# Four-layer attention and state-space stack on one core: first-forward kernel tiles in the attention core, a re-ordered first spectral block, and POOL's work re-dealt

## The chip, the cores and the metric

The kernel runs on one core of one Trainium2 chip. A core has five engines that run side by side, each from its own list of instructions: PE (matrix products; results go to PSUM, accumulation memory of eight banks), DVE (vector operations), ACT (scalar functions, copies and casts), POOL (general work; it can also issue DMA transfers) and SP (here it issues DMA transfers only). Engines wait for one another by semaphores. An engine takes its instructions strictly in order, so one that waits holds everything queued behind it on the same engine. "Evacuation" is a copy out of PSUM into on-chip memory by DVE or ACT, usually with a change of layout or type.

The metric is the time of one execution in microseconds (us), as the median of several runs; lower is better.

## The reference

The input x has 2048 positions of 512 channels in bf16. Two layers A and B alternate, A B A B, each with a layer-norm before it and a residual addition behind it. Both passes use the same weights.

```python
def _A_ref(x, wqkv, wo):                 # 32 heads of 16 channels
    q, k, v = ...                        # x @ wqkv, split
    idx = pos[:, None] - off[None, :]    # off = 0, 2, 4, ... 14
    logits = einsum("bhsd,bhswd->bhsw", q, kg) * scale   # masked where idx < 0
    attn = softmax(logits)
    return einsum("bhsw,bhswd->bhsd", attn, vg) @ wo

def _B_ref(u, A_re, A_im, B_re, B_im, C_re, C_im, log_dt, Dskip):
    P = exp((dt * A)[:, :, None] * l)              # 512 channels x 128 states x 2048 positions
    K = einsum("dn,dnl,dn->dl", Cc, P, dt * Bc).real
    Kf, Uf = rfft(pad(K, 4096)), rfft(pad(u, 4096))
    return irfft(Uf * Kf)[:2048] + u * Dskip

x = x + _A_ref(_layernorm(x)); x = x + _B_ref(_layernorm(x), ...)
x = x + _A_ref(_layernorm(x)); x = x + _B_ref(_layernorm(x), ...)
```

Layer A lets each position look at itself and at seven earlier ones, two apart. Layer B is a convolution over the whole length with a kernel K per channel, done with a Fourier transform.

## The kernel before

The stages follow each other, with overlaps at their seams; times are from the start of the span.

0 to 106 us, `k_gen` with ORDERK. The kernel K is computed once, from tables of powers (`A_t`, `B_t`) whose products are summed by PE over the states (`pk`), evacuated by ACT (`kgs`) and stored as bf16 to the scratch tensor `kd_dram` by `k_store` (L1331): four groups of six transfers, 24 in all. Interleaved with it is the front of the first layer A: layer-norm, transposes, and the projections of k and of the first q. It works on a reduced set of 641 positions; `k_load` later expands them to 2048.

106 to 186 us, the first attention core, `LayerA.core` with CORE0. A letter is one step; q runs over four quarters of the positions, ft over four quarters of the channels:

- `m` is a DVE product of q and k (`prod`, L342), `l` its sum on PE (L350 and L354), `x` the maximum (DVE), `e` exponentials (ACT), `r` the reciprocal of the sum (two ACT operations), `n` the normalization (DVE), `T` a transpose;
- `v` is a value projection on PE with its ACT evacuation (L400), sixteen in all. After the fifteenth and the sixteenth, two transfers each shift copies of v by rows (L403) for the window; those of the first are ahead of all the rest in the queue;
- `q` is a projection of q (L223) with its ACT evacuation (L225);
- `P` is a product of the weights and the values (`pav`, L467; DVE), `S` and `V` its sum over the window (PE, then an ACT evacuation), `O` the output projection with the residual (PE, ACT), and `b`, `d`, `a`, `f` are the layer-norm that follows, the input `u` of layer B.

The digits and capitals in CORE0 are steps of the coming block: `0` the index arithmetic of a table of sines (`indices`, eight iotas and eight multiplications of 128 x 512 int32 on POOL, L736 and L737); `2` to `5` the sines on ACT, stored to `g2_dram`; `1` and `6` the loads of the two channel halves of K (`k_half_load`); `8` and `9` one row's addition of Dskip on DVE (`k_half_fix`); `A` to `H` the copies of K into `k_perm` on ACT or DVE (`k_part`); `w` the load of a 4 MB table of Fourier factors, `w2_dram`, in four transfers (`load_w2`, L598).

186 to 241 us, the first spectral block, `FftB.run` with ORDER0. The Fourier transform of 4096 is factored into two steps. `K` and `U` are tiles of the first forward step of the kernel and of the input (`f1`: 16 matrix products of 128 x 64 outputs, one evacuation L798 of 128 x 1024, by ACT where the token ends in A, by DVE where it ends in D). Sixteen tiles of each exist, eight per half of the channels, and a half's spectrum is the 16 KB tile `a1s` (per partition). `k` and `u` are the second step (L809 or L816; the evacuation of `k` by the token's letter, that of `u` by ACT, L867). `m` is the DVE product of the spectra (`u_mult`); it also stores the kernel's spectrum to `kf_dram`, from which the second block loads it again. `y` and `Y` are the first inverse step, `w` and `z` the second, with a residual addition.

Seven steps are left over from the first core and are put in behind the first seven K tiles after the first, in the order LATE0: the end of one layer-norm group and its four rows on POOL (`a`), statistics of the rows 14 and 15 (`s`, `t`), their gathering (`g`), the reciprocal (`r`), the last group and its four rows on POOL (`b`), and two masks (`m`).

241 to 270 us, ORDERF: the end of the block's second half, with the front of the second layer A. 270 to 352 us, the second attention core with CORE1; there `w` loads the same table again. 352 to 397.5 us, the second spectral block with ORDER1, which makes only the input's spectrum.

What sets the order. The strings are executed token by token, and every instruction of a token goes behind the earlier ones of its engine: DVE, ACT, PE and SP have exactly the order of the strings, in the generator POOL too. After that POOL's instructions are placed by the compiler's own scheduler. Nearly all loads and stores of `before` are issued by SP, so a transfer that waits in SP's list holds the ones behind it. The `kr` pool holds the two halves `k_rl0` and `k_rl1` and the Dskip row until the core's end, `krctx2.close()`.

The lines which the steps below speak of most:

```python
dsk = krp.tile([1, D], BF16, name="dskip")
nc.sync.dma_start(dsk[:], ins["Dskip"].partition_broadcast(1))
...
late = la.core(x_sb, u, lnp, CORE0, ev, 3)
late["m"] = C["masks"]
krctx2.close()
...
fb.run(ORDER0, u, k=kp, late=[late[c] for c in LATE0.split()])
```

Of the kernel before, what the change touches and what calls it, by code (L numbers as in the profile page):

```python
# [10 lines left out]
ACT = mybir.ActivationFunctionType  # L11
ALU = mybir.AluOpType
# [8 lines left out]
P = 128  # L21
# [57 lines left out]
NCOL = (2, 2)  # L79
PRELOAD = (slice(0, 0), slice(5, 16))  # L80
# [119 lines left out]
class LayerA:  # L200


    def __init__(self, tc, nc, consts, lnst, A_wqkv, A_wo, layer, xnT, nq):
# [11 lines left out]
        self.ps_l = self.wv = None  # L215
# [143 lines left out]
    def core(self, x_sb, u, lnp, order, ev, nprod=0):  # L359
# [9 lines left out]
        with ExitStack() as c2:  # L369
# [17 lines left out]
            def pq_tile():  # L387
                return ps_q.tile([P, 512], F32, name="pq", tag="pq")

# [187 lines left out]
            if l == 0:  # L577
                out_proj(15)
                return {"a": lambda: [u_end(8), u_apply(8, range(8, 12), "pool")], "s": lambda: x_stats(14), "t": lambda: x_stats(15),
                        "g": lambda: u_aggr(12, 16), "r": lambda: u_rstd(12),  # L580
                        "b": lambda: [u_end(12), u_apply(12, range(12, 16), "pool")]}
# [11 lines left out]
    def load_w2(self, w2_dram):  # L593
# [3 lines left out]
        for c in range(4):  # L597
            self.nc.sync.dma_start(self.w2[:, c * 32:(c + 1) * 32, :], w2_dram[:, c * 32:(c + 1) * 32, :])  # L598
# [128 lines left out]
def build_g2(nc, tmp, p21, g2_dram, room):  # L727
# [4 lines left out]

    def indices(h):
# [13 lines left out]
class FftB:  # L747
# [38 lines left out]
    def spectrum(self, g, key):  # L786
        if g == (key == "ua"):
            return self.gtile("a1s")
# [832 lines left out]
```

## Time and profile before

| | |
|---|---|
| time, median of three runs | 399.32 us (399.11, 399.32, 401.1) |
| the profiled execution: time, span | 399.32 us, 397.5 us |
| mean granted clock of PE | 0.983 |
| busy: PE | 344.0 us (87%) |
| busy: DVE | 378.7 us (95%) |
| busy: ACT | 328.6 us (83%) |
| busy: POOL | 54.4 us (14%) |
| DMA | 54.17 MB, 62322 packets, mean 136 GB/s |

The span reaches from the first to the last instruction of the trace; the time of the execution is 1.8 us longer. "Busy" counts an engine's arithmetic instructions. In a row of busy groups stand the line, the engine, the operation, its output and inputs by name, their shapes, the count, the busy time and the mean of one in ns, and then the idle time of the engine ahead of them with what ended it. In a row of the timeline stand the start in us, the duration, the engine, the line and the instruction; "x3" means three in a row with their time together. A row of the table by stage has the window, its length, and the busy time and count of each engine. A row of DMA issues has the tile, the queue, the count, KB of each and the median time from issue to landing.

### The profile page before, as it was taken

To read this page: it belongs to the slowest core of one execution; us is meant where nothing else is said; L and a number is where in the kernel's file an instruction comes from. 1 tells how busy PE (TensorE), PEld (TensorE's weight loads), DVE (VectorE), ACT (ScalarE), POOL (GpSimd) and SP (SyncE) were. 2 spreads that over 40 slices of the span, in tenths; PEclk is the share of its full clock that TensorE was granted. 3 is DMA by queue.
4 is the path that set the end of the run, shared out by engine and by line. 5 is a ranking of instruction groups with operands and counts; after the bars stand their busy time and mean duration, and the time that the engine had idled before them with its cause. 6 is when DMAs were issued, how large, how long until landed. Compare 5 with 4: busy or idle time off the path is not lost.

```text
span 397.5 us, 14823 instructions
## 1 busy us (share of the span) xinstructions
PE 344.0 (87%) x6510; PEld 236.8 (60%) x6556; DVE 378.7 (95%) x452; ACT 328.6 (83%) x585; POOL 54.4 (14%) x75
## 2 busy tenths in 40 slices
PE   3855589799999979889998889999999998887895
PEld 2221237477535667657887888543456676566885
DVE  6999999999999999999999998979999999989994
ACT  7999989999566588988999987675566889989974
POOL 9303000000399302001500000100000001000000
PEclk9998869999999999999999999999999999999999
DMA  7953610314114754278137485820153037504506
GB/s 213 399 155 48 71 54 2 92 29 95 41 42 120 205 181 151 73 243 347 63 123 265 177 293 164 295 77 1 41 159 93 5 119 309 162 3 142 181 11 207
DMA packets 62322, 54.17 MB, mean 136 GB/s; under 512 B 33869, under 2 KB 50738, under 8 KB 60978
## 3 DMA queue, kind: packets, MB, share of 16 engines
q1 hardware_dynamic: 62250, 53.22, 43.7%
q8 instruction: 51, 0.84, 0.9%
q14 instruction: 13, 0.11, 0.1%
q10 hardware_dynamic: 8, 0.00, 0.0%
HBM read 30.15 MB, written 13.24 MB: 109 GB/s over the span
## 4 chain that ended last, share of the span: by engine, by line
PE 39%; ACT 25%; DVE 20%; issue 6%; SPq 4%; DMA 4%; POOL 1%; DVEq 0%; ACTq 0%; POOLq 0%
PE pq L398 7%; PE pq L223 5%; DVE pav L467 4%; PE pp L282 3%; ACT ln_junk L145 3%; PE pk L1309 3%; SPq L1414 3%; ACT ub L867 2%; PE pb L816 2%; PE pp L1247 2%; PE L L350 2%; DMA w_sb<-w_dram 2%; ACT ln_junk L1195 2%; ACT a1s L798 2%; DVE A_t L1143 2%
## 5 line engine op out<-in xcount | busy, mean ns | idle before, releaser
L467 DVE TENSOR_TENSOR pav<-attn,v_ext 128x4096 bf16<-128x4096 bf16 (+1 forms) x34 | 72.4, 2167 | 0.2
L342 DVE TENSOR_TENSOR prod<-qT,kT_ext 128x4096 bf16<-128x4096 bf16 x29 | 66.5, 2326 | 1.0 <-PE L L350 1.0
L1143 DVE TENSOR_TENSOR A_t<-A_t,pow_t 128x1024 bf16<-128x1024 bf16 (+4 forms) x46 | 38.1, 870 | 0.4
L492 PE MATMUL po<-ident,pav 64*128 64x64 bf16 x1664 | 29.1, 190 | 6.6 <-DVE pav L467 3.7
L492 PEld LDWEIGHTS <-pav 64*128 64x128 bf16 x1664 | 26.3, 95 | 14.3 <-DVE pav L467 10.3
L867 ACT CAST ub<-pb 128x1024 bf16<-128x1024 f32 x32 | 32.0, 1077 | 1.2 <-PE pb L816 1.2
L509 PE MATMUL pq<-wop,oT 128*128 128x512 bf16 x116 | 30.9, 380 | 2.3 <-issue 1.4
L816 PE MATMUL pb<-a1s,w_sb 128*128 128x64 bf16 x768 | 27.6, 193 | 5.0 <-ACT a1s L798 1.7
L398 PE MATMUL pq<-wv,xnT 128*128 128x512 bf16 x122 | 30.0, 380 | 0.3
L400 ACT CAST v_ext<-pq 128x512 bf16<-128x512 f32 x32 | 18.8, 587 | 13.4 <-PE pq L398 13.4
L816 PEld LDWEIGHTS <-w_sb 128*128 128x128 bf16 x768 | 24.9, 98 | 7.3 <-issue 5.2
L798 ACT CAST a1s<-pb 128x1024 bf16<-128x1024 f32 x29 | 28.1, 1057 | 0.8 <-PE pb L809 0.8
L1309 PEld LDWEIGHTS <-A_t 128*64 128x64 bf16 (+1 forms) x512 | 21.7, 103 | 5.6 <-issue 1.2
L1309 PE MATMUL pk<-B_t,A_t 128*64 128x84 bf16 (+1 forms) x512 | 23.6, 201 | 1.5 <-ACT kgs L1317 1.0
L225 ACT CAST qT<-pq 128x512 bf16<-128x512 f32 x24 | 14.1, 587 | 13.1 <-PE pq L223 13.1
L1247 PE MATMUL pp<-xnT,kT_ext 128*128 128x512 bf16 x87 | 22.8, 384 | 1.5 <-ACT kT_ext L1252 0.4
L798 DVE CAST a1s<-pb 128x1024 bf16<-128x1024 f32 x19 | 22.6, 1215 | 1.4 <-PE pb L809 1.3
L223 PE MATMUL pq<-xnT,kT_ext 128*128 128x512 bf16 x89 | 23.2, 380 | 0.4
L1111 PE MATMUL pt<-ws,ident 128*128 128x512 f32 x16 | 11.5, 811 | 13.7 <-ACT ws L1098 13.3
L398 PEld LDWEIGHTS <-xnT 128*128 128x128 bf16 x128 | 11.7, 98 | 14.7 <-issue 2.1
L509 PEld LDWEIGHTS <-oT 128*128 128x128 bf16 x128 | 11.8, 98 | 13.1 <-ACT oT L494 1.9
L809 PE MATMUL pb<-F1c,xnT 128*64 128x128 bf16 x256 | 17.8, 219 | 1.5 <-ACT ub L867 0.6
(274 smaller groups left out, 904.4 us busy)
## 6 DMA issues: line engine op xcount, KB each, us to landing
w_sb<-w_dram SPq DMA_DIRECT2D x8, 1024.0 KB, 7.8
w_dram<-xnT SPq DMA_DIRECT2D x1, 4096.0 KB
kf_ring<-kf_dram SPq DMA_DIRECT2D x13, 256.0 KB, 4.4
kf_ring<-kf_dram SPq DMA_DIRECT2D x26, 128.0 KB, 3.6
v_ext<-v_ext SPq DMA_DIRECT2D x4, 784.0 KB, 6.1
x_blk<-in_A_x_dram SPq DMA_DIRECT2D x4, 512.0 KB, 4.2
kT_ext<-in_A_wqkv_dram SPq DMA_DIRECT2D x4, 512.0 KB, 9.5
x_sb<-in_A_x_dram SPq DMA_DIRECT2D x4, 512.0 KB, 5.6
```

Source lines behind the costliest of these rows:

```text
L223: nc.tensor.matmul(pq[:], lhsT=self.wqk[:, dt, ft * P:(ft + 1) * P], rhs=self.xnT[:, dt, q * 512:(q + 1) * 512], start=(dt == 0), stop=(dt ...
L342: nc.vector.tensor_tensor(pr, self.qT[q][:, ft].unsqueeze(1).to_broadcast([P, W, 4, P]), kap, ALU.mult)
L398: nc.tensor.matmul(pp[:], lhsT=xnT[:, dt, a * P:(a + 1) * P], rhs=wv[:, dt, :], start=(dt == 0), stop=(dt == NDT - 1))
L467: nc.vector.tensor_tensor(pv[:, i], attn[:, n % 4].unsqueeze(2).to_broadcast([P, W, DH // parts, H]), vap, ALU.mult)
L492: nc.tensor.matmul(po[:, h, 0, i * nt + ft, :], lhsT=pvf[rows, i, w, ft * P:(ft + 1) * P], rhs=ident[rows, rows], start=(w == 0 and ft + i ...
L509: nc.tensor.matmul(pw[:], lhsT=oT[:, ftp, :], rhs=self.wo[:, ftp, :], start=False, stop=(ftp == NDT - 1), skip_group_check=ahead)
L798: (self.nc.scalar.copy if eng == "act" else self.nc.vector.tensor_copy)(dst, src)
L816: nc.tensor.matmul(p2[:, j, :], lhsT=self.w2[:, ec * EC + j, :], rhs=a1s[:, ec * EC + j, :], start=True, stop=True)
L867: nc.scalar.copy(ub[:], p2)
L1143: return lambda: nc.vector.tensor_tensor(*args)
L1247: nc.tensor.matmul(pps[kind, b, ft][:], lhsT=la.wqk[:, dt, c:c + P], rhs=la.xnT[:, dt, b * 512:(b + 1) * 512], start=(dt == 0), stop=(dt = ...
L1309: nc.tensor.matmul(o, lhsT=lhs, rhs=Bt[:, ri, c * CH + ql].rearrange("p b g -> p (b g)"), start=(not half and j % 4 == 0 and ri == 0), sto ...
```

## The change

Five things change together.

1. Four of the sixteen first-forward tiles of the kernel spectrum (KEARLY = 4) are made inside the first attention core. A new step `*` in CORE0 (`k_f1`) makes half a tile: eight matrix products into one PSUM bank of the pool that the core's projections use, `pq`, and one ACT copy of 128 x 512 into `a1s`. Eight `*` stand near the end of CORE0. ORDER0 has the twelve other K tiles. `a1s` lies now in the `kr` pool: one 16 KB tile holds both halves of the loaded K, then `a1s` of the kernel, then that of the input ("a1u"); the pool is closed after the block. With both halves in one tile, `1` and `6` stand side by side in CORE0.
2. The late layer-norm steps are tokens of ORDER0 (`a`, `s`, `t`, `g`, `r`, `e`, `c`, and `q` for the masks) in place of LATE0. The eight rows are single tokens: c4 on DVE, c5 on ACT, the other six on POOL.
3. The multiplications of the index arithmetic move from POOL to ACT: `0` is only the eight iotas, and the new steps `W`, `X`, `Y`, `Z` are two ACT operations each, in CORE0.
4. Transfers: half of the kernel's stores (groups 0 and 2, twelve of 24) are issued by POOL; the stores to `kf_dram` are issued by POOL, at the kernel's second step and not at the product; the table `w2_dram` is loaded in sixteen transfers in place of four, four per `w` token, with four `w` in CORE0 and in CORE1.
5. ORDERK, ORDER0, CORE0 and CORE1 are written in another order. The steps of ORDERK and of CORE1 are the same but for the three more `w` in CORE1. In ORDER0 DVE evacuates 6 K and 8 k tiles (before: 7 and 9), ACT 6 and 8 (9 and 7).

The diff, cut to its core:

```diff
 ORDERK = """
-sibCCiisbisCCCiiMMbsGiCMMiMMbbMMsTbGiiscbbccMMbiTisbTTbGGGcGTTTiTTGiiTTTsGbibbGGGasTcMMMMaiiaaaa
-aasMMTiillWaTlbyMMwMyyayMMaMMMbattseeMMMiiMMMMkkMMMMMkkbKHqqKaqqppaaQadxaUUUUUUUkkllxUWppaQUUKlq
-UqyUUUqqyyHyQxttkkTTTTTpdeeKTTTTQT3qqqqaaQkkQaakkKTaallqxqpWEQx333KxlTTykkkppTkyyyxxHtUUeKUUtppl
-kUUeUKkxkkUWpUlzKzzzxkkttKkeKekpUUUUUKkkkkUUUEUUxUKEqxppKooxqXkxkQpKkkoXXKpZZZxx
+CisibCsiibsCCCbiiisMCMMMMMMibbGcTsbiiGsMMcbbbMciiGsTTTTbbTTiiTTasTiiGGGcbbTTTbcMGGGsMMaMaaaaaaii
+sTTGGlliiWMMlbsMMyyyyibiwMMMtteeqqMMMMbQdMMMMMMkkaaKMMkMMkakMakHKqKqaaaqaUpUUpQUUUqUllUWxxplpyyy
+ayUQkkxKttdqHaeUUUUUTqeaQqqqQxaaTaqT33TTTapkkTTTKpTa3QllWqqTlTxxykykTTKyQppkyxH3lkktkeUUxWKUUtpU
+lxzzppzEzektKxxkkkKEKteepkkkkKKkkkUUkUUUUUUEKKUoUUUUkkkoKkoUUpxxqqKQppxXXXpZZxxZ
 """
 ORDER0 = """
-KD KA KA KA KD KA KD KA KD KA KD kA KA kD KA KD UA KD UA UA UD KA kA kD kA UD UA UD UA kD kA kD u UD
-u u UA m m m UA u u UD u UA m kD UA kD UA m m u UA u m kA u kD u m kD u kD kA kA yA m YA m yD u yA u
-m m m u u yA m m u YA m yA w000D yD yA YD yA w010D YA yD yA
+q a c0 s KD c1 KA KD t g KA KD KA r c3 e c7 KD KA c4D c2 c6 c5A kA kD kA kD kA KA KD UA KD UA UA UD
+KA UD UA UD UA kD kA u kD u UD m UA UA kA UD UA u m kD kA m u u kD m u UA m UA UA m kD u u u m kD u
+kA kA m m m u u u m m yA YA yD u m m u u m yA yA YA m w000D yA yD yA YD yA YA yD yA w010D
 """
-LATE0 = "a s t g r b m"
...
 CORE0 = """
-vmvvvlmqlxmvvvemlvqrlmqvnTmlvxqqlmevlrvmmvvvvnPllPqxmSqTeO0mPlVrP15SOS2PnOPVPOSml4qOOlb3mV78lPPC
-SOdxS6eOrPSPPOSnwaOPSBPOSaOS9bOfAPdbFPOtVftEGDSaafaOH
+mmvv0lvvmxvvllveqqrvYmmlnlmmvqTvvlWxvvvevmvrZq16XPllPqn5Sqml2mq4VTO3xPPSPl8qOmSPOV7ePOS9lOrVPmOn
+SPOOmSllwPBxEPADOGSeOSCrPFwHOwwn*SP****bPS*ObPSdaaf*fdOVbO*aafPSttaO
 """
 CORE1 = """
-0vm2m1llqqq3mmlqvlmmvvvllvxemmqvrvllqqnTvvmmxlqvvvvvmlvPPeqlrmqmlxSqnqSmTPPOOSelSPPpOSrOSmOOlPPS
-mppSOOnlPlppxSeOPwpbbrVPddffaSfOOPnVPpfPSpOSPpafbOSOppPttSdfafaaO
+0mv12m3llmmqqqlqvlvmmvxvllmvevqrmvnllqqTvvmmlqlxmmvPPvvvvveqlmlqxmqSrnOSTpPPOlSeSrPOSOPSPPOSqlpO
+SpmmOlOplnpPSxPeObbPdrpwVffaSfdOOPnVPPpfSpOSPpObafPSwOtppSdfwafwtaOa
 """
+KEARLY = 4
...
     def load_w2(self, w2_dram):
-        for c in range(4):
-            self.nc.sync.dma_start(self.w2[:, c * 32:(c + 1) * 32, :], w2_dram[:, c * 32:(c + 1) * 32, :])
+        def piece(i):
+            for c in range(4 * i, 4 * i + 4):
+                self.nc.sync.dma_start(self.w2[:, c * 8:(c + 1) * 8, :], w2_dram[:, c * 8:(c + 1) * 8, :])
+        return iter([lambda i=i: piece(i) for i in range(4)])
+
+    def w2_next(self, w2_dram):
+        if self.w2_parts is None:
+            self.w2_parts = self.load_w2(w2_dram)
+        next(self.w2_parts)()
...
+    def iotas():
+        for h in range(4):
+            for k in range(2):
+                g = gi[h][:, k * 4 * P:(k + 1) * 4 * P]
+                nc.gpsimd.iota(g.rearrange(...), pattern=[[8, 4], [128, P]], base=32 * h, channel_multiplier=0)
+
     def indices(h):
         for k, bias in enumerate((16384.0, 32768.0)):
             g = gi[h][:, k * 4 * P:(k + 1) * 4 * P]
-            nc.gpsimd.iota(g.rearrange(...), pattern=[[8, 4], [128, P]], base=32 * h, channel_multiplier=0)
-            nc.gpsimd.tensor_scalar(g, g, p21, bias, ALU.mult, ALU.add)
+            nc.scalar.activation(g, g, ACT.Identity, scale=p21, bias=bias)
...
     def kf_load(self, n):
             for h in range(2):
                 sync.dma_start(kc[h::2, 1], kc[1 - h::2, 0])
+            self.nc.gpsimd.dma_start(self.kf_dram[g, ec].rearrange("p r q e -> (p r) (q e)"), kc[:, 0].rearrange("p q e -> p (q e)"))
             return
...
     def u_mult(self, g, ec):
         if self.tag == 0:
-            self.nc.sync.dma_start(self.kf_dram[g, ec].rearrange("p r q e -> (p r) (q e)"), kc[:, 0].rearrange("p q e -> p (q e)"))
             self.free.append(kc)
...
-                    nc.sync.dma_start(dst, sr)
+                    (nc.sync if g % 2 else nc.gpsimd).dma_start(dst, sr)
...
     def k_half_load(h):
-        kr = krp.tile([P, NA, D // 2], BF16, name=f"k_rl{h}")
-        k_load(tc, nc, kr, kd, hs)
-        krs[h] = kr
+        if h == 0:
+            krs["both"] = krp.tile([P, 2, NA, D // 2], BF16, name="k_rl", tag="kr")
+        krs[h] = krs["both"][:, h]
+        k_load(tc, nc, krs[h], kd, hs)
...
+    def k_spectrum(name="a1s"):
+        return krp.tile([P, P * DQG], BF16, name=name, tag="kr")[:]
+
+    def k_f1():
+        i = krs["n"] = krs.get("n", -1) + 1
+        if i == 0:
+            krs["a1s"] = k_spectrum().rearrange("p (e q) -> p e q", q=DQG)
+        p1 = la.pq_tile()
+        for j in range(4):
+            lhs = kp[:, i * 4 + j].rearrange("p a r -> p (a r)")
+            for half, m in enumerate((C["F1c"], C["F1s"])):
+                nc.tensor.matmul(p1[half * 64:(half + 1) * 64, j * P:(j + 1) * P], lhsT=lhs, rhs=m[:], start=(j == 0), stop=True, skip_group_check=True)
+        nc.scalar.copy(krs["a1s"][:, :, i * 4:(i + 1) * 4], p1[:].rearrange("p (q e) -> p e q", q=4))
...
-    late["m"] = C["masks"]
-    krctx2.close()
+    late["q"] = C["masks"]
...
+    fb.S[0]["ka"], fb.cnt["K"], fb.one = krs["a1s"], KEARLY - 1, k_spectrum
     with tc.manual_schedule(engines=MAN):
-        late["."] = lambda: None
-        fb.run(ORDER0, u, k=kp, late=[late[c] for c in LATE0.split()])
+        fb.run(ORDER0, u, k=kp, more=late)
     fb.c_mid.close()
+    krctx2.close()
```

More of the change, by code (lines that the diff above doesn't have):

```diff
@@ L388, in pq_tile @@
                 return ps_q.tile([P, 512], F32, name="pq", tag="pq")
+            self.pq_tile = pq_tile
             def q_proj(q, ft):
@@ L761, in __init__ @@
         self.nkf = 0
+        self.nk = self.one = None
         g2p = self.c_grp.enter_context(tc.tile_pool(name=f"b{tag}_g2", bufs=1, reuse_waits="tile"))
@@ L787, in spectrum @@
         if g == (key == "ua"):
-            return self.gtile("a1s")
+            return self.one("a1u") if self.one else self.gtile("a1s")
         if self.pair is None:
@@ L935, in i2_cols, with run @@
             nc.scalar.copy(xr, p4[:])
-    def run(self, order, u, done=lambda g, t: None, k=None, late=(), more={}):
-        late, cnt = list(late), self.cnt
+    def run(self, order, u, done=lambda g, t: None, k=None, more={}):
+        cnt = self.cnt
         src = dict(K=("ka", k), U=("ua", u))
-        if not cnt:
+        if self.nk is None:
             self.nk, self.nm = (0, 0) if k is not None else (NG * NEC, 0)
@@ L967, in run @@
                 if op == "K":
-                    if n > 0 and late:
-                        late.pop(0)()
                     if n == NG * NQT - 1:
```

21 lines of the change are left out of this document (10 added, 11 removed).

## The prediction

> **What bounds the kernel now.** I read the page's busy times first, then the busy times by stage, then what VectorE (DVE) waited for, and then the lines of the stretch that the change touches.
>
> ```profile
> span 397.5 us, 14823 instructions
> PE 344.0 (87%) x6510; PEld 236.8 (60%) x6556; DVE 378.7 (95%) x452; ACT 328.6 (83%) x585; POOL 54.4 (14%) x75
> 106.00:140.00 34.00, 33.27 (x389) 16.80 (x388) 33.52 (x20) 20.04 (x35) 26.12 (x16) 1.00 0.46 120
> 140.00:186.00 46.00, 41.50 (x1063) 30.18 (x1074) 45.45 (x44) 40.16 (x89) 3.01 (x1) 1.00 0.58 191
> 186.00:244.00 58.00, 52.36 (x1521) 47.51 (x1521) 56.32 (x70) 53.68 (x61) 6.41 (x9) 1.00 0.56 195
> 0.00:106.00 106.00, 78.75 (x740) 45.85 (x753) 100.33 (x162) 97.13 (x193) 16.16 (x47) 0.94 0.44 111
> 270.00:352.00 82.00, 75.67 (x1521) 46.67 (x1532) 80.42 (x67) 62.88 (x137) 1.02 (x1) 1.00 0.33 108
> DVE prod L342 <- PE L L350: 1.0, 2, 0.5
> DVE kn L798 <- PE pb L816: 0.7, 2, 0.5
> ```
>
> The stage rows give window, length, then busy time of PE, PEld, DVE, ACT, POOL. DVE is the engine without slack: 135.3 of 138 us busy from 106 to 244 us, the first attention core and the first spectral block, where nearly all of the change lies. No wait of DVE there is longer than 0.5 us. So what leaves DVE's list shortens the span, as long as ACT and PE still deliver on time. They have little to give: PE is full in the first 34 us (33.3 busy), ACT in the last 58 (53.7 busy). Only ACT before 140 us is idle, 14 of 34 us.
>
> **The change part by part.** The sum goes against the profiled execution, 397.5 us of span and 399.32 us of time, which is the median of the three runs.
>
> (1) Early first-forward tiles and the re-dealt evacuations. The block order has twelve K tiles for sixteen: one DVE evacuation of a K tile less (seven to six), three of ACT less (nine to six). Of the second-step evacuations DVE has one less (nine to eight), ACT one more. Late layer-norm rows: POOL six for eight, DVE and ACT one more each.
>
> ```profile
> 194.92 3.61 DVE L798 CAST a1s<-pb 128x1024 bf16<-128x1024 f32 x3
> 184.97 1.06 DVE L197 TENSOR_SCALAR xnT<-x_sb,ln_rstd,ln_nb 128x512 bf16<-128x512 bf16 x3
> 193.49 5.60 ACT L798 CAST a1s<-pb 128x1024 bf16<-128x1024 f32 x6
> L195 ACT ACTIVATE xnT<-x_sb,ln_nb,ln_rstd 128x512 bf16<-128x512 bf16 x3 | 2.4, 816 | 0.0
> L400 ACT CAST v_ext<-pq 128x512 bf16<-128x512 f32 x16 | 9.4, 586 | 6.9 <-PE pq L398 6.9
> 160.00:186.00 26.00, 22.77 (x51) 1.00 0.66 222
> ```
>
> In rows an evacuation follows the next after 1.13 to 1.20 us on DVE and 0.93 on ACT. DVE: 2 x 1.13 - 0.33 = 1.93 us less. ACT in the block: 3 x 0.93 - 0.93 - 0.82 = 1.0 us less. The eight half tiles add 8 x 0.59 = 4.7 us of ACT at the end of the core (row of the equal-sized evacuation of v_ext). From 160 to 186 us ACT has 26 - 22.8 = 3.2 us free, so up to 1.5 us of it could stick out there, and the block takes 1.0 of that back; I count 0, with 1.5 us as the upper end. The matmuls are the same in number and only move.
>
> (2) The index arithmetic goes from POOL to ACT.
>
> ```profile
> 112.63 7.10 DVE L342 TENSOR_TENSOR prod<-qT,kT_ext 128x4096 bf16<-128x4096 bf16 x3
> 120.26 2.70 DVE L342 TENSOR_TENSOR prod<-qT,kT_ext 128x4096 bf16<-128x4096 bf16 x1
> 124.02 7.13 DVE L342 TENSOR_TENSOR prod<-qT,kT_ext 128x4096 bf16<-128x4096 bf16 x3
> 131.67 4.89 DVE L467 TENSOR_TENSOR pav<-attn,v_ext 128x4096 bf16<-128x4096 bf16 x2
> 142.02 6.68 DVE L467 TENSOR_TENSOR pav<-attn,v_ext 128x4096 bf16<-128x4096 bf16 x3
> 105.80 1.19 POOL L736 IOTA g_i<- 128x512 int32 x2 [67.48 <-PE pk L1309]
> 113.63 7.20 POOL L737 TENSOR_SCALAR g_i<-g_i,aux 128x512 int32<-128x512 int32 x2
> 125.21 7.01 POOL L737 TENSOR_SCALAR k_perm<-k_perm,aux 128x512 int32<-128x512 int32 x2
> L663 ACT ACTIVATE w_qi<-w_base,w_off,pk 128x512 int32<-128x512 int32 x1 | 0.9, 867 | 0.0
> ```
>
> While POOL multiplies (107 to 132 us) three products of equal size take 7.10 and 7.13 us against 6.68 later, one takes 2.70, and two 4.89 against 4.48: 0.42 + 0.42 + 0.45 + 0.41, about 1.7 us of DVE that should go, since the POOL multiplications go and only writing iotas stay. The Trainium skill ("SBUF — State Buffer", Who interferes with whom) says that a DVE instruction with two SBUF inputs contends with a GpSimd instruction that reads SBUF, not with one that only writes; the trace agrees, with the 2.70 us.
>
> ACT gets eight operations of 0.59 (v_ext's row) to 0.87 us (the one int32 row), 4.7 to 6.9 us in its 14 idle ones. But two of them stand ahead of a q evacuation. The new DVE list reaches its first PV product after one product and one normalization less than before: 131.67 - 2.28 - 0.60 - 1.25 (slow products) = 127.5 us, and the product that needs that q (two PV products of 2.23 and a normalization later) at 132.6. PE is full until then, so the last value projection comes only by what was taken from ahead of it: two q projections and a logit sum,
>
> ```profile
> 132.82 0.59 ACT L400 CAST v_ext<-pq 128x512 bf16<-128x512 f32 x1 [0.28 <-PE pq L398]
> 123.23 1.89 PE L223 MATMUL pq<-xnT,kT_ext 128*128 128x512 bf16 x8
> 127.06 0.94 PE L354 MATMUL L<-ind,prod 128*128 128x8 bf16 x32
> ```
>
> 2 x 0.86 + 0.8 = 2.5 us, to 130.3 for its evacuation. Then come the reciprocal (to about 132.3), two index operations and the q evacuation: 132.3 + 1.2 + 0.6 = 134.1 us, 1.4 us late. I charge DVE 1.4 us (2.0 with the 0.87 row, 0 if PE runs ahead of this count).
>
> (3) Half of the kernel stores go to POOL's queue.
>
> ```profile
> 106.37 15.81 SPq L1331 DMA_DIRECT2D kd_dram<-kgs  x24
> 123.28 0.23 SPq L1475 DMA_DIRECT2D dskip<-in_B_Dskip_dram  x1
> 123.57 0.69 SPq L403 DMA_DIRECT2D v_ext<-v_ext  x1
> v_ext<-v_ext SPq DMA_DIRECT2D x4, 784.0 KB, 6.1
> 121.84 2.35 POOL L737 TENSOR_SCALAR k_perm<-k_perm,aux 128x512 int32<-128x512 int32 x2
> ```
>
> SP keeps twelve of the 24 (7.9 us, to 114.3) and then stands at the dskip load, which waits for every kernel store, POOL's twelve too; behind it are queued the v_ext shift of the first PV products, the output weights, x and both kernel halves. No POOL-issued transfer is in this trace. Bounds for one: 0.66 us, SP's own issue (15.81 / 24), and 1.2 us, POOL's multiplication at its quickest (2.35 / 2), or 2.35 if it costs as much as a pair of them. I take the 0.66, being the same transfers. POOL starts after two iotas at 107.0; with some 2 us until the last lands, SP goes on at 107.0 + 12 x 0.66 + 2 = 117 us, and the shift lands at 117 + 0.3 + 6.1 = 123.4, before 127.5: no wait. At 1.2 us it lands at 129.8: 2.3 us. The Trainium skill ("DMA: Bandwidth & Descriptors", Latency and other measured facts) gives about 1 µs to the first byte of a POOL-issued transfer; by that as the price of one, an estimate, the shift would land at 127.4 and the sum stay as it is.
>
> (4) Both kernel halves are loaded back to back, and the second Dskip addition follows the first by 6.6 us on DVE, not 18.
>
> ```profile
> 133.43 0.64 SPq L403 DMA_DIRECT2D v_ext<-v_ext  x1
> 138.38 1.55 SPq L1398 DMA_DIRECT2D k_rl<-kd_dram  x1
> 139.97 11.78 SPq L1414 DMA_DIRECT2D k_rl<-kd_dram  x17
> DMA to landing us min/median/max: 3.5/5.3/7.1
> ```
>
> From the second shift to the end of one half SP needs 151.75 - 133.43 = 18.3 us, so the second half's first load goes at 130.3 + 18.3 = 148.6 and lands at 152.1 to 155.7. DVE wants it at 127.5 + 24.1 = 151.6, with the 1.4 us of (2) at 153.0: 0 to 2.7 us. I take 0: the 3.5 is that of the load with no x load ahead of it.
>
> (5) At nothing: the sixteen kf stores moved from SP to POOL (POOL has 6.4 us of work in the block's 58, and buffers come free earlier; the next layer's memset behind them on POOL is not early in its need); the w2 load in 32 smaller issues, 12 us more of SP in all, half in each layer. Its cover:
>
> ```profile
> 171.68 3.24 SPq L598 DMA_DIRECT2D w_sb<-w_dram  x4
> L816 PE MATMUL pb<-a1s,w_sb x302: 189/193/203, 191.9 to 215.0; 128*128 128x64 bf16 x151
> w_sb<-w_dram SPq DMA_DIRECT2D x8, 1024.0 KB, 7.8
> ```
>
> Issued to 174.9 and landed some 8 us on, it is first used at 191.9: 9 us of cover, against 6 us of added issue. The new orders of the kernel generator and of the second core hold the same instructions; DVE's idle time there is 5.7 and 1.6 us, so they can win 2 or 3 us at most and lose as much: 0.
>
> The sum: 399.3 - 1.9 - 1.7 + 1.4 = **397.1 us**.
>
> **The rivals.**
>
> POOL's queue holds SP (slower). Place: the dskip load. At a price p per transfer the shift lands at 107.0 + 12p + 8.4; the wait reaches the 3.6 us won at p = 1.32. At 1.6 it is 7.1 us, which takes the place of the 1.4: 399.3 - 3.6 + 7.1 = 402.8; at 2.35 it is 411.8. The first index operation on ACT waits for the same POOL queue. For it: dispatch by a software engine beside a busy DVE. Against: DVE runs two-input products then, not copies. The Trainium skill ("SBUF — State Buffer", the box on DVE blocking DMA) says that descriptors of POOL-issued transfers are not written while DVE is in a two-port mode, which it grants to copies, casts and tensor_scalar, not to tensor_tensor; by it the stores in the core are safe. No run here shows it yet. Chance 0.20.
>
> The gain arrives at DVE and is lost to ACT and loads (no change): ACT's 1.5 us of (1), the 0.87 row in (2) and 0.9 us of (4) at the median landing: 397.1 + 1.5 + 0.6 + 0.3 = 399.5; with one of them 398.5. Chance 0.13.
>
> A new order costs in the generator or the second core (slower): the generator runs ACT 97.1 of 106 us, so a DVE step moved 3 to 6 us ahead of the ACT step that it needs waits that long: 397.1 + 4.5 = 401.6. Against: the same steps, each moved little. Chance 0.12.
>
> The change not doing what it says: the half tiles share two PSUM banks with the output projections; if these then wait, nothing leaves the block early. This falls under the second rival.
>
> **How the numbers follow.** My forecast has 0.55, in 394.5 to 398.4 (the orders' 2.6 us below; 1.3 above). Within 0.5% of 399.3 (397.3 to 401.3), about what a measurement of this kernel can tell from no change, lie 0.12 of the forecast and the second rival; below it the other 0.43; above it the first and third, 0.32. Range: 394.0 to 404.0; what is left out is the tail of the first rival and better orders.
>
> **What would show it.** Products of 2.2 us at 107 to 132 us, none of 2.7. The dskip load on SP before 118 us, and a DVE wait ahead of the first PV product below 1 us. A DVE wait of about 1.4 us some 5 us later, on ACT's q. The first block's f1 evacuations ending some 2 us sooner relative to its first. Wrong if DVE waits on a v_ext shift or on the index operations for over 3 us, or if DVE's idle time from 0 to 106 us grows over 8 us.

## The result, and the profile after

The changed kernel takes 405.09 us (median of six runs, 403.62 to 407.03), the kernel before, in runs beside it, 401.17 us (399.11 to 404.58). The ratio is 1.0121 with a 95% interval of 1.0092 to 1.0150: slower by about 1.2%, where 397.1 us and a gain of 0.6% had been forecast. The profiled execution took 403.62 us, the shortest of its six and 4.3 us more than that of before.

The page's busy times, and then the busy times by stage of the changed kernel (window, length, then PE, PEld, DVE, ACT, POOL, granted clock, DMA share, GB/s):

```profile
span 401.8 us, 14890 instructions
PE 346.1 (86%) x6510; PEld 236.7 (59%) x6556; DVE 376.5 (94%) x451; ACT 335.7 (84%) x600; POOL 45.3 (11%) x93
140.00:186.00 46.00, 39.31 (x997) 27.60 (x1006) 39.60 (x37) 36.10 (x83) 3.02 (x1) 0.96 0.53 159
105.86:248.90 143.04, 128.25 (x2969) 95.06 (x2985) 132.46 (x129) 120.91 (x199) 27.03 (x43) 0.99 0.59 183
```

The last row goes from the first core product behind the generator to the first step of the second layer's layer-norm. The same stretch of the kernel before:

```profile
106.97:244.44 137.47, 126.65 (x2965) 94.62 (x2981) 134.77 (x130) 113.94 (x184) 34.57 (x25) 1.00 0.55 176
```

That is the account of the 4.3 us. The generator ends 1.11 us earlier. From there to 248.9 us DVE has 2.31 us less work (134.77 to 132.46), where 3.6 had been forecast, but stands idle 10.58 us in place of 2.70. The rest of the span is 0.16 us shorter. So work was saved, and 7.9 us of new waiting ate it. Most of the waiting falls in the first core: from 140 to 186 us DVE is idle 6.4 of 46 us, 0.55 before. What DVE waited for longest in the whole stretch, from the waits of the changed kernel (engine, line, what ended the wait; total, times, longest in us):

```profile
DVE attn L450 <- ACT rs L442: 3.8, 1, 3.8
DVE k_rl L1502 <- DMA k_rl<-kd_dram: 1.4, 1, 1.4
DVE z L814 <- PE pb L901: 1.3, 1, 1.3
DVE ln_bn L138 <- ACT x_sb L516: 0.8, 1, 0.8
```

The longest is followed back on the timeline, in order: ACT's last sine, SP's list, then ACT, PE and DVE (start, duration, instruction, and in brackets the idle time ahead of it and what ended it):

```profile
142.00 1.04 ACT L756 ACTIVATE k_perm<-g_i 128x1024 bf16<-128x1024 int16 x1
135.67 12.52 SPq L1428 DMA_DIRECT2D k_rl<-kd_dram  x17
148.24 0.61 SPq L1412 DMA_DIRECT2D k_rl<-kd_dram  x1
148.89 10.69 SPq L1428 DMA_DIRECT2D k_rl<-kd_dram  x17
159.69 2.62 SPq L757 DMA_DIRECT2D g_dram<-k_perm  x4
167.14 1.99 ACT L1506 COPY k_perm<-k_rl 128x1024 bf16<-128x1024 bf16 x2 [4.17 <-DMA w_sb<-w_dram]
171.00 1.89 PE L511 MATMUL pq<-wop,oT 128*128 128x512 bf16 x4 [3.75 <-ACT oT L496]
176.14 0.31 ACT L442 ACTIVATE rs<-ssum 128x128 bf16<-128x128 f32 x1
176.49 0.69 DVE L450 TENSOR_TENSOR attn<-ex,rs 128x1024 bf16<-128x1024 bf16 x1 [3.80 <-ACT rs L442]
```

The sines are made in the room of `k_perm`, and from there stored to `g2_dram`; the copies of the kernel may write `k_perm` only when those stores have landed. All four sines are ready at 143 us. Their stores stand on SP behind both kernel halves, 36 transfers, and go at 159.7 to 162.3 us; they take 4 to 4.9 us to land. ACT's first copy waits 4.17 us. The profile names a transfer of the table there, which landed at the same time; by the program the copy waits for the sine stores. Everything behind the copy on ACT waits with it: an evacuation that PE needs (3.75 us), the exponentials of the last quarter, and so DVE's normalization (3.80 us). And PE's clock drops behind its pause, shown by the same windows in steps of 2 us:

```profile
168.00:170.00 2.00, 0.00 (x0) 0.00 (x0) 2.00 (x5) 1.97 (x5) 0.00 (x0) 1.00 1.01 358
170.00:172.00 2.00, 1.00 (x3) 0.44 (x4) 2.00 (x2) 1.87 (x4) 0.00 (x0) 0.60 1.05 388
172.00:174.00 2.00, 2.00 (x55) 1.18 (x54) 0.69 (x3) 1.04 (x3) 0.00 (x0) 0.55 1.00 344
174.00:176.00 2.00, 1.87 (x38) 1.05 (x29) 0.00 (x0) 1.97 (x5) 0.00 (x0) 1.00 1.01 357
```

The granted clock (the third number from the end) was 0.55 to 0.60 for 4 us after the pause of 3.75 us, so PE's next matrix products took up to twice as long: four of 128 x 512 took 1.89 us, where the same four take 1.03 us at other times.

### The profile page after: what moved, and what is told of

Its sections match the earlier page's. It is cut to its first block, busy times and chain, and to the rows that moved or that the text cites. A ratio compares the mean times of both kernels' runs of the same rounds, so it can differ in the third digit from the quotient of the medians.

```text
span 401.8 us, 14890 instructions
## 1 busy us (share of the span) xinstructions
PE 346.1 (86%) x6510; PEld 236.7 (59%) x6556; DVE 376.5 (94%) x451; ACT 335.7 (84%) x600; POOL 45.3 (11%) x93
## 4 chain that ended last, share of the span: by engine, by line
PE 40%; DVE 26%; ACT 18%; issue 6%; DMA 5%; SPq 3%; POOL 1%; DVEq 0%; ACTq 0%; POOLq 0%
PE pq L400 7%; DVE pav L469 6%; PE pk L1323 4%; PE pq L223 4%; PE pp L1261 4%; PE pp L282 3%; DMA k_rl<-kd_dram 3%; DVE A_t L1157 3%; DVE B_t L1157 2%; ACT ub L883 2%; ACT a1s L814 2%; DVE prod L342 2%; PE L L350 2%; PE po L494 2%; PE pq L511 2%
## 5 line engine op out<-in xcount | busy, mean ns | idle before, releaser
L342 DVE TENSOR_TENSOR prod<-qT,kT_ext 128x4096 bf16<-128x4096 bf16 x29 | 65.2, 2283 | 0.7 <-PE L L350 0.5
L1261 PE MATMUL pp<-xnT,kT_ext 128*128 128x512 bf16 x88 | 24.9, 413 | 5.4 <-ACT xnT L1254 3.5
L832 PE MATMUL pb<-a1s,w_sb 128*128 128x64 bf16 x640 | 23.2, 193 | 4.7 <-ACT ub L883 1.3
L178 POOL TENSOR_TENSOR ln_rstd<-ln_rstd,ln_mh 128x4 f32<-128x4 f32 x2 | 4.1, 2028 | 144.3 <-DVE ln_msq L170 80.3
L814 DVE CAST a1s<-pb 128x1024 bf16<-128x1024 f32 x16 | 18.9, 1217 | 1.5 <-PE pb L825 1.3
L814 ACT CAST a1s<-pb 128x1024 bf16<-128x1024 f32 x20 | 19.4, 1041 | 1.0 <-PE pb L825 0.9
```

The costliest lines, as they stand in the source:

```text
L342: nc.vector.tensor_tensor(pr, self.qT[q][:, ft].unsqueeze(1).to_broadcast([P, W, 4, P]), kap, ALU.mult)
L814: (self.nc.scalar.copy if eng == "act" else self.nc.vector.tensor_copy)(dst, src)
L832: nc.tensor.matmul(p2[:, j, :], lhsT=self.w2[:, ec * EC + j, :], rhs=a1s[:, ec * EC + j, :], start=True, stop=True)
L1261: nc.tensor.matmul(pps[kind, b, ft][:], lhsT=la.wqk[:, dt, c:c + P], rhs=la.xnT[:, dt, b * 512:(b + 1) * 512], start=(dt == 0), stop=(dt = ...
```

## The experiments

The theory after reading the two traces: SP's list. With both halves loaded back to back, the sine stores start 8 us later than in the kernel before, and ACT, PE and DVE wait in turn. Rivals: the transfers are crowded by the table's sixteen loads, and the store's place matters little; or the early half tiles fill ACT and PSUM at the core's end. Ratios below are to the kernel before, with runs of the same group. Each group of four had its own runs of before, so a difference between groups is less sure than one within a group.

**E1: sine stores on POOL.** Only their queue changes.

```diff
-        nc.sync.dma_start(g2_dram[:, :, h * 4:(h + 1) * 4, :], gs...)
+        nc.gpsimd.dma_start(g2_dram[:, :, h * 4:(h + 1) * 4, :], gs...)
```

> The changed kernel, with the four stores of the sine table issued by POOL in place of SP, nothing else. Theory 1, SP's queue: in the changed kernel these stores stand behind both kernel halves on SP (issued at 159.7 to 161.7 us, the sines were ready from 135.5 to 143.1), ACT's first copy into k_perm, the room in which the sines lie, waits 4.17 us for them, PE 3.75 us behind ACT, DVE 3.80 us behind PE. It expects the stores to go before 146 us, ACT's wait below 0.5 us, DVE's wait on the last normalization below 0.5 us, PE's granted clock at 1.00 from 170 to 175 us (0.66 in the changed kernel), DVE's 1.4 us wait on the second half's load unchanged, and a ratio to before of 1.012 less 3.8 to 4.6 us in 401, 1.000 to 1.003. Rival, crowded transfers: ACT really waits for a landing that the sixteen table loads hold up; then its wait stays over 2 us and the ratio at 1.010 to 1.013. Rival, early tiles: the half tiles fill ACT at the core's end; then DVE's wait on the last normalization stays over 2 us.

Measured: 1.0049 (1.0032 to 1.0067), above the 1.000 to 1.003 expected. The timeline of this kernel, and last the row of its stretch from the first core product to the second layer's layer-norm:

```profile
144.56 0.69 POOL L757 DMA_DIRECT2D g_dram<-k_perm  x1 [3.47 <-ACT k_perm L756]
154.63 0.28 DVE L1502 TENSOR_TENSOR k_rl<-k_rl,dskip 1x256 bf16<-1x256 bf16 x1 [1.45 <-DMA k_rl<-kd_dram]
164.14 1.99 ACT L1506 COPY k_perm<-k_rl 128x1024 bf16<-128x1024 bf16 x2
173.84 0.68 DVE L450 TENSOR_TENSOR attn<-ex,rs 128x1024 bf16<-128x1024 bf16 x1
189.43 0.69 DVE L138 BATCH_NORM_STATS2 ln_bn<-x_sb 128x6 f32<-128x512 bf16 x1 [1.49 <-ACT x_sb L516]
106.79:247.03 140.24, 127.67 (x2969) 94.77 (x2985) 132.40 (x129) 121.23 (x199) 29.75 (x47) 1.00 0.58 184
```

ACT's copies and DVE's normalization have no wait left, PE's granted clock stays at 1.00 from 168 to 176 us, and 0.7% of the 1.2% is back, some 2.9 us. The rivals would have kept the waits. The gain is a little below the 3.8 us expected, for one of the next waits grew: for row 14's output projection from 0.83 to 1.49 us. DVE is still idle for 7.84 us of this stretch (140.24 less 132.40), against 2.70 in the kernel before: the sine stores were the longest wait and not the only one.

**E2: second half behind the sines, on SP.** Step `6` goes behind the last sine, and its Dskip addition `9` ahead of the copies that need it.

```diff
-...rZq16XPllPqn5Sqml2mq4VTO3xPP...7ePOS9lOrVPmOn
+...rZq1XPllPqn5Sqml2mq4VTO36xPP...7ePOSlOrVPmOn
-SPOOmSllwPBxEP...
+SPOOmSllwPBx9EP...
```

> The changed kernel, with the load of the second kernel half put behind the sine stores on SP, and its Dskip addition after the last maximum on DVE, just ahead of the copies that need it. Theory 1, SP's queue: the stores go from 148 to 151 us, ACT's first copy into k_perm does not wait for them, the second half is issued from 151 to 162 us and lands by 166; what can wait now is ACT's second copy (the first of the second half), 0 to 3 us. DVE's waits of 1.4 us (second half) and 3.8 us (last normalization) go or fall to below 2 us together. Ratio to before 0.997 to 1.005. Rivals (transfers crowded by the table's loads; early tiles filling ACT): 1.008 to 1.013.

Measured: 1.0074 (1.0048 to 1.0099), above what I expected of the theory, and as near to the rivals' 1.008 to 1.013; the timeline has to decide.

```profile
148.38 3.56 SPq L757 DMA_DIRECT2D g_dram<-k_perm  x4
152.67 9.83 SPq L1428 DMA_DIRECT2D k_rl<-kd_dram  x17
166.21 1.05 ACT L1506 COPY k_perm<-k_rl 128x1024 bf16<-128x1024 bf16 x1 [2.95 <-DMA k_rl<-kd_dram]
173.74 0.69 DVE L450 TENSOR_TENSOR attn<-ex,rs 128x1024 bf16<-128x1024 bf16 x1 [2.89 <-ACT rs L442]
```

The stores go in time and the first copy waits no more; now the second copy waits 2.95 us for the half that stands behind them, and DVE 2.89 us. The mechanism holds, but I had called 3 us of ACT's wait and less than 2 us of DVE's. The new order of the core wants both within the same few us, and neither of the two orders of SP's list gives both; the second queue of E1 does, and helps more.

**E3: E1, and the second Dskip addition one product later.**

```diff
-...7ePOS9lOrVPmOn
+...7ePOSlOrVP9mOn
```

> The sine stores issued by POOL as in the first kernel, and the second Dskip addition one product later on DVE, so that its 1.4 us wait on the second half's load is covered. Theory 1 expects 0.8 to 1.4 us below the first kernel: ratio to before 0.997 to 1.001, and no DVE wait of over 1 us from 107 to 235 us. If the wait only moves, DVE's idle time in the core stays as in the first kernel and the ratio with it.

Measured: 1.0015 (0.9994 to 1.0035), 0.3% below E1, as the covering of a 1.4 us wait would give, and the kernel stands level with before. With the stores on a second queue and the addition later the loss is gone; the forecast gain is not there. The profiled execution of E3 was the longest of its twelve (404.72 us, median 400.46), so its trace can't show what the others waited for; the trace of E7 below, which has the addition at the same place, shows no wait of DVE on the second half.

**E6: the changed kernel without early tiles.** KEARLY is 0, the `*` go, and three K tiles for ACT and one for DVE come back into ORDER0.

```diff
-KEARLY = 4
+KEARLY = 0
-n*SP****bPS*ObPSdaaf*fdOVbO*aafPSttaO
+nSPbPSObPSdaaffdOVbOaafPSttaO
-q a c0 s KD c1 KA KD t g KA KD KA r ...
+q KA KD a c0 KA s KD c1 KA KD KA t g KA KD KA r ...
```

> The changed kernel without early tiles: all sixteen kernel tiles in the block (seven evacuated by DVE, nine by ACT, as in the kernel before), no half tiles in the core. Theory 1, SP's queue: ACT's 4.2 us wait and DVE's 3.8 us wait in the core stay, the block is 1 to 2.5 us longer, ratio to before 1.014 to 1.019. Rival, the half tiles fill ACT and two PSUM banks at the core's end and cost the time: the waits fall below 2 us and the ratio to 1.000 to 1.005.

Measured: 1.0161 (1.0130 to 1.0193). DVE's wait on the reciprocal stays (4.7 us), as the theory has it. The early tiles did not cost the time: without them it is 0.4% longer still.

**E9: E3 without early tiles**, the same edit on the kernel of E3.

> The changed kernel with the sine stores on POOL and the later Dskip addition, without early tiles: all sixteen kernel tiles in the block, evacuated seven by DVE and nine by ACT. If the early tiles are a gain once the wait in the core is away (one DVE evacuation of 1.13 us and three of ACT's leave the block), the ratio is 1.003 to 1.007 against 1.0015 with them. If what they take out of the block comes back as DVE's 1.5 us wait on ACT at the core's end, the ratio is 1.000 to 1.002 and that wait is gone.

Measured: 1.0062 (1.0036 to 1.0088) against 1.0015 (0.9994 to 1.0035) with them, in another group; the intervals just miss each other. With E6 that puts the early tiles at about 0.4 to 0.5%, some 1.6 to 1.9 us, but not all of it need be theirs. The longest wait of DVE in this trace, 2.24 us, stands some 25 us ahead of where the early tiles are made in E1: PE had stopped for 1.50 us in a logit sum (the last section comes back to this stop), and its granted clock was 0.50 from 145 to 148 us. The wait at the core's end is another one here, in the second row:

```profile
148.56 2.29 DVE L469 TENSOR_TENSOR pav<-attn,v_ext 128x4096 bf16<-128x4096 bf16 x1 [2.24 <-PE po L494]
189.02 1.23 DVE L814 CAST a1u<-pb 128x1024 bf16<-128x1024 f32 x1 [1.89 <-PE pb L825]
```

With the early tiles (E1) DVE waits 1.49 us where the core ends and the block begins, without them 1.89.

**E4: E3 with all kernel stores on SP.**

```diff
-                    (nc.sync if g % 2 else nc.gpsimd).dma_start(dst, sr)
+                    nc.sync.dma_start(dst, sr)
```

> The version with the sine stores on POOL and the later Dskip addition (ratio 1.0015), with all 24 kernel stores on SP again. If POOL's twelve stores are a gain, as the prediction's working has it (SP free 7.9 us sooner), then SP reaches the shift of v_ext about 7 to 8 us later, near 126 us, it lands near 132 us, DVE's first value product (126.4 us) waits 4 to 7 us, and the ratio is 1.011 to 1.021. If the shift was hidden anyway, or if POOL's stores cost what they save, the ratio is 0.998 to 1.005.

Measured: 1.0084 (1.0050 to 1.0118); E7 and E8 below, of the same group and with POOL's stores, have 1.0045 and 1.0030. The timeline:

```profile
122.64 0.69 SPq L405 DMA_DIRECT2D v_ext<-v_ext  x1
129.48 4.49 DVE L469 TENSOR_TENSOR pav<-attn,v_ext 128x4096 bf16<-128x4096 bf16 x2 [2.98 <-ACT ssum L441]
```

SP issues the shift 4.0 us later (118.60 in the changed kernel), it lands at 128.8 us, and DVE's first value product, which needs it, waits 2.98 us. The profile names an ACT step that ended about then; the program has the shift. The sign is as expected, the size is about half, and the interval overlaps those of E7 and E8. Some of the time may be PE's: it waits 2.38 us for a product of DVE, and its granted clock is 0.53 and 0.61 in the steps from 138 to 142 us. SP reaches the dskip load 6.0 us later than in the changed kernel (122.34 against 116.36 us), but there the shift was not ready behind it: it also waits for a value projection's evacuation, which ends at 118.58 us.

**E5: E3 with the index multiplications on POOL.**

```diff
-            nc.scalar.activation(g, g, ACT.Identity, scale=p21, bias=bias)
+            nc.gpsimd.tensor_scalar(g, g, p21, bias, ALU.mult, ALU.add)
```

> The same base, with the eight index multiplications on POOL again. If two-input DVE work and reading POOL work slow each other, as the prediction's working has it, three to five DVE products of 107 to 132 us take 2.6 to 2.7 us in place of 2.28, DVE's busy time grows by 1.2 to 1.7 us, and the ratio to 1.004 to 1.006. If ACT's eight added operations cost as much elsewhere, the ratio stays at 1.000 to 1.003 though the products are slow.

Measured: 1.0070 (1.0045 to 1.0095). Three pairs of two-input operations on DVE take 4.89 or 4.90 us where pairs beside them take 4.49, 1.2 us in all and the least that was expected, and POOL suffers more than DVE:

```profile
118.77 4.90 DVE L342 TENSOR_TENSOR prod<-qT,kT_ext 128x4096 bf16<-128x4096 bf16 x2
129.66 8.05 POOL L752 TENSOR_SCALAR k_perm<-k_perm,aux 128x512 int32<-128x512 int32 x2
137.75 1.06 ACT L756 ACTIVATE k_perm<-k_perm 128x1024 bf16<-128x1024 int16 x1 [3.30 <-POOL k_perm L752]
```

Two multiplications of POOL take 8.05 us here, 2.35 at their quickest in the kernel before, and ACT's first sine waits 3.30 us for them. Behind it an evacuation comes late, PE stands 1.87 us, its granted clock is 0.50 from 139 to 145 us, and DVE waits 2.37 and 1.43 us for PE: more than the slow products cost. So in the new order of the core the indices would be late on POOL, and the move is needed as much as it is useful. The interval overlaps E7's.

**E7: E3 with row 14's statistics behind the first K tile on DVE; E8: E7 with the residual addition `w010D` four steps earlier.**

```diff
-q a c0 s KD c1 KA KD t g ...
+q a c0 KD c1 KA s KD t g ...
-w000D yA yD yA YD yA YA yD yA w010D
+w000D yA yD yA YD w010D yA YA yD yA
```

> The same base, with the statistics of row 14 behind the first kernel tile's evacuation on DVE and those of row 15 where they stood relative to it. DVE waits 1.5 us for that row in the base, because ACT reaches the last rows' copies later with the half tiles among them. If this is ACT's overflow at the core's end, the wait is covered by the evacuations: DVE's wait there falls below 0.5 us and the ratio by 0.002 to 0.004, to 0.998 to 1.000. If the block's first tiles are late as well (they need the same PE and ACT), DVE waits for them in its place and the ratio stays at 1.000 to 1.003.

> The kernel with the later statistics, and besides it the second residual addition of the block's first half four steps earlier, where DVE otherwise waits 1.2 us for PE. If this wait is only a matter of order, 0.5 to 1.2 us go: 0.001 to 0.003 below the kernel with the later statistics, 0.995 to 0.999 to before. If PE is the bound there, the wait moves and the ratio is the same.

Measured: 1.0045 (1.0023 to 1.0067) and 1.0030 (0.9995 to 1.0064): no gain that can be told from E3, and E7 above both ranges that I had named. The waits moved. From the timeline of E7:

```profile
187.85 1.23 DVE L814 CAST a1s<-pb 128x1024 bf16<-128x1024 f32 x1 [1.99 <-PE pb L825]
```

In E8 the later of the two residual additions waits 1.30 us for PE, where an evacuation waited 1.25 us in the changed kernel. DVE is ready before PE at both seams. To put another DVE step first does not help.

**F1: the kernel before, with the second half loaded right behind the first.** One thing of the change alone.

```diff
-...VrP15SOS2PnOPVPOSml4qOOlb3mV78lPPC
-SOdxS6eOrPSPP...
+...VrP165SOS2PnOPVPOSml4qOOlb3mV78lPPC
+SOdxSeOrPSPP...
```

> The kernel before with one thing of the change: the load of the second kernel half right behind the first on SP, ahead of the sine stores; all else as before. If the sine stores' place is what costs, they now go near 164 to 166 us (151.9 to 159.6 before), land near 168, and ACT's first copy into k_perm (161.4 us before) waits 4 to 7 us; some of it reaches DVE, which waits for the last normalization's reciprocal: ratio 1.005 to 1.015. If the place in SP's list does no harm by itself (DVE has other work, or the rest of the change is needed for the wait), the ratio is 0.998 to 1.003.

Measured: 1.0207 (1.0166 to 1.0247), more than I expected. Timeline, and one of the windows:

```profile
154.52 10.38 SPq L1414 DMA_DIRECT2D k_rl<-kd_dram  x17
165.02 2.61 SPq L742 DMA_DIRECT2D g_dram<-k_perm  x4
170.42 1.04 ACT L1491 COPY k_perm<-k_rl 128x1024 bf16<-128x1024 bf16 x1 [7.74 <-DMA g_dram<-k_perm]
172.00 1.89 PE L492 MATMUL po<-ident,pav 64*128 64x64 bf16 x64 [7.31 <-ACT oT L494]
173.92 2.29 DVE L467 TENSOR_TENSOR pav<-attn,v_ext 128x4096 bf16<-128x4096 bf16 x1 [5.98 <-PE po L492]
178.53 2.29 DVE L467 TENSOR_TENSOR pav<-attn,v_ext 128x4096 bf16<-128x4096 bf16 x1 [2.31 <-PE po L492]
170.00:175.00 5.00, 3.00 (x67) 2.16 (x67) 1.08 (x1) 3.54 (x8) 0.00 (x0) 0.50 0.98 377
```

Here the profile names the sine stores itself. One token moved in the kernel before makes ACT wait 7.74 us, PE 7.31 and DVE 5.98, and then 2.31 more, while PE is back at half its clock: the same 64 matrix products took 1.89 us at 172 and 1.11 at 177. So the store's place is enough to cause the loss (F1), and mending it takes most of the loss away (E1).

**F2: the kernel before, with the index multiplications on ACT** (`0` only iotas, and `Y`, `W`, `Z`, `X` between the value projections). **F3: F2 with the changed kernel's ORDERK.**

```diff
-vmvvvlmqlxmvvvemlvqrlmqvnTmlvxqqlmevlrvmmvvvvnPllPqxmSqTeO0mPlVrP15...
+v0mvvvlmqlxmvvvemlvqrYlmqvnTmlWvxqqlmevlrZvmmvvvvnXPllPqxmSqTeOmPlVrP15...
```

> The kernel before with another thing of the change alone: the index multiplications on ACT, in four pairs between the value projections, POOL only writing. If reading POOL work slows two-input DVE work, the three slow products and the two slow value products return to 2.28 and 2.24 us, 1.2 to 1.7 us of DVE, and with ACT idle 14 of 34 us there the ratio is 0.996 to 0.998. If ACT's pairs delay the evacuations that PE and DVE wait for, the ratio is 0.999 to 1.002.

> The second kernel of this group (index multiplications on ACT) with the changed kernel's order of the generator. In the changed kernel's trace the core's first product starts 1.1 us earlier (105.86 against 106.97 us). If that is the order's own gain, 0.5 to 1.1 us go: 0.001 to 0.003 below the second kernel, 0.993 to 0.996 to before. If it comes from half the kernel stores leaving SP, or varies with the clock, the ratio is that of the second kernel.

Measured: 0.9996 (0.9972 to 1.0021) and 0.9979 (0.9955 to 1.0004). The groups of F2, and three rows of its timeline:

```profile
L342 DVE TENSOR_TENSOR prod<-qT,kT_ext 128x4096 bf16<-128x4096 bf16 x13 | 29.3, 2285 | 1.1 <-ACT qT L225 0.6 <-PE L L350 0.5
119.89 0.69 DVE L445 TENSOR_TENSOR ex<-ex,rs 128x1024 bf16<-128x1024 bf16 x1 [0.33 <-ACT rs L440]
126.73 4.49 DVE L342 TENSOR_TENSOR prod<-qT,kT_ext 128x4096 bf16<-128x4096 bf16 x2 [0.61 <-ACT qT L225]
142.26 4.49 DVE L467 TENSOR_TENSOR pav<-attn,v_ext 128x4096 bf16<-128x4096 bf16 x2 [0.44 <-DMA v_ext<-v_ext]
```

The products are all at 2.28 us again, so reading POOL work did slow them. But DVE, with 1.4 us less work, now waits 0.33, 0.61 and 0.44 us at three places, and no gain is measured; the interval leaves room for one of up to 0.3%. The first wait is for a reciprocal that ACT delivers as far behind the first core product as before. The other two come mostly of ACT delivering later: counted from that product, the evacuation of q comes 0.48 us and the last one of the values, on which the shift of `v_ext` waits, 1.31 us later than in the kernel before, each behind a pair of index operations (1.34 and 1.32 us) that now stands ahead of it on ACT. So here it was the moved work itself, more than the old pace of PE and ACT, that took the gain back, and a better place for the pairs was not tried. F3 has the lowest ratio of all kernels here, and its interval just reaches 1: whether the generator's new order is worth anything in the time can't be said. The traces speak for a small gain: the first core product stands at 106.97 us in the kernel before, 107.22 in F2 and 108.26 in F1, at 106.48 in F3, and at 105.84 to 106.79 in the changed kernel and the nine made from it, with all kernel stores on SP (E4, 105.93) as well as without. No version clearly beats both kernels.

## Why the prediction was wrong

The forecast was 397.1 us, in 394 to 404; the median was 405.09, and the ratio puts it at 399.3 x 1.0121 = 404.2 beside the earlier runs of before. The direction was wrong.

The step that failed is (4). It followed the second half to its landing and asked only when DVE wants it. That much came out: the first load was forecast for 148.6 and went at 148.24, the landing fell in its bounds, and DVE's wait was 1.44 us, in the 0 to 2.7 given and taken as 0 (E3 puts it at 0.3%). What (4) left out is what is queued behind the moved loads: the four sine stores, which in the kernel before go between the halves (from 151.85 us). The question what the queue holds behind a transfer was asked of the dskip load and not of these. Through ACT and PE that cost DVE 3.80 us and PE its clock; E1 and F1 show it from both sides. This accounts for 0.7% of the 1.2% lost. With E3's 0.3% the kernel is level with before, so the other error is in the sum of (1) and (2): it took 3.6 us off the span. DVE's list lost 2.31, and with the stores mended (E1) DVE is still idle for 5.1 us more in that stretch than in the kernel before.

(1) The evacuations: right in the main. Two DVE evacuations fewer, as counted; but the late rows on DVE took 2.8 us for six, beside POOL's rows, against 1.9 for five, so the added row cost 0.9 us where 0.33 was taken. E9 against E3 puts the early tiles at about 0.5%, where 1.93 us were forecast, with the reserve named at E9. The 1.5 us of ACT's overflow, taken as 0, was there: 0.83 us in the changed kernel, 1.49 in E1.

(2) The products: right in size on DVE's list, wrong in worth. The groups of the kernel before and then of the changed kernel, from 100 to 249 us:

```profile
L342 DVE TENSOR_TENSOR prod<-qT,kT_ext 128x4096 bf16<-128x4096 bf16 x13 | 30.5, 2379 | 0.4 <-PE L L350 0.4
L467 DVE TENSOR_TENSOR pav<-attn,v_ext 128x4096 bf16<-128x4096 bf16 x15 | 34.0, 2304 | 0.0
```

```profile
L342 DVE TENSOR_TENSOR prod<-qT,kT_ext 128x4096 bf16<-128x4096 bf16 x13 | 29.3, 2282 | 0.2
L469 DVE TENSOR_TENSOR pav<-attn,v_ext 128x4096 bf16<-128x4096 bf16 x15 | 34.0, 2284 | 1.0 <-PE po L484 0.7
```

They lost 1.2 and 0.3 us; 1.7 was the forecast. The wait on ACT's q, charged with 1.4 us, did not come. But the sum treated each us off DVE's list as one off the span, though it had itself noted PE at 33.3 of 34 us there. In F2 the 1.4 us came back as waits, mostly behind the index operations on ACT, which the prediction had charged only at one q evacuation. How much of it would be kept with ACT on time, no run shows.

(3) POOL's queue: right, and the first rival, which rested on it, wrong. Twelve stores took 6.86 us, 0.57 each, below the 0.66 taken; from the changed kernel's timeline:

```profile
106.19 6.86 POOL L1345 DMA_DIRECT2D kd_dram<-kgs  x12
116.36 0.23 SPq L1489 DMA_DIRECT2D dskip<-in_B_Dskip_dram  x1
118.60 0.69 SPq L405 DMA_DIRECT2D v_ext<-v_ext  x1
126.35 4.48 DVE L469 TENSOR_TENSOR pav<-attn,v_ext 128x4096 bf16<-128x4096 bf16 x2
```

The dskip load was forecast for 117 us and the first value product for 127.5, without a wait. E4 gives what POOL's share is worth, about half of what was expected and less surely. The rule of the Trainium skill on DVE blocking POOL-issued transfers ("SBUF — State Buffer", the box on DVE blocking DMA) was not put to the test: the `kf_dram` stores took 0.54 to 0.62 us each to issue beside DVE's casts, but these casts read PSUM, and no run shows that they were in the two-port mode of which the rule speaks.

(5) and the third rival: the second core cost nothing (0.16 us less from 248.9 us on), none of DVE's waits in the block names a `kf_dram` store, and the generator ended 1.1 us earlier, where a loss was the rival. The second rival named waits that came (ACT's overflow, the second half), at smaller sizes than the one that decided.

## What to carry to other kernels

When a transfer moves in an in-order queue, list what now stands behind it, and follow each of those to its reader; the one that is moved past matters more than the one that moves. A copy that may only overwrite a buffer after a store has landed is a reader like any other, though no data flow shows it: look for rooms that two uses share. And a us taken from the busiest engine is a us of the span only where what it needs next comes as much earlier; if the moved work stands ahead of that on another engine, or that engine is full too, it becomes a wait.

## What the runs showed that I had not expected

PE pays twice for a pause. After 3.75 us of idle time the granted clock was 0.55 to 0.60 for 4 us, after 7.31 us it was 0.50 for at least 5 us, and pauses of about 1 us left it at 1.00. The Trainium skill ("TensorE: Matmul & The Clock Gate", Part 1) says that the clock is halved after at least one idle window of some 3.4 us, and is given back after as long a busy one; these two pauses agree, and so does E2's (3.39 us, then 0.51 to 0.64 for 4 us). Shorter pauses do not: 2.87 us (E3), 2.38 (E4), 1.87 (E5) and 1.50 us (E9) also cost the clock, while another of 1.50 us (E6) left it at 1.00. Read in steps of 0.2 us, the clock was at 0.50 for 3.4 us at a time (the changed kernel, E2, E4, E6, E9) or twice that (6.8 us in E3 and E5) or three times (10.2 us in F1), and of the 3.4 us ahead of it PE had been idle for 1.1 (E5) to 3.2 us (the changed kernel). So the length of the window agrees, but by these measurements PE need not be idle for all of it; what does decide is left open. A wait of 7.7 us on ACT became 8.3 us on DVE this way (F1).

In most of the changed kernels PE stops within one logit sum, thirteen of its 32 matrix products done, with nothing waited for that the profile shows ("issue"): here the changed kernel.

```profile
143.01 0.63 PE L354 MATMUL L<-ind,prod 128*128 128x8 bf16 x19 [0.95 <-issue]
```

It is always the same instruction, for 0.4 to 1.5 us and 2.87 us in the profiled execution of E3, and neither the kernel before nor E4, E5 and F1 to F3 have it there. It is not free: in E9 and E3 PE's clock was halved behind it, and DVE then waited 2.24 and 3.8 us. The transfers are at 1.01 of their engines from 135 to 140 us in the changed kernel, 0.98 before, and at 0.26 from 140 to 145 us, when PE stops, so crowding alone does not explain it. Its cause was not tried and is left open.
